# Linear attention before a mixture of experts: block transposes on VectorE, products in quarters of the array, and PSUM in four pairs of banks

## The chip, the core and the metric

The kernel runs on one core of a Trainium2 chip. The metric is the device time of one execution in microseconds (us). A core has five engines with in-order queues of their own: TensorE (PE, its weight loads shown apart as PEld), VectorE (DVE), ScalarE (ACT), GpSimd (POOL) and SyncE (SP, which here only issues DMA transfers). Engines wait for one another by semaphores. TensorE writes into PSUM, 8 banks of 512 fp32 per partition.

## The reference, cut to what matters

Attention first, in fp32, with 8 batches b, 8 heads h, 576 tokens s, head width d = 64 and 128 features f:

```
def phi(x):                                    # x: q or k
    proj = einsum('bhsd,df->bhsf', x, w_phi)
    proj = proj - max(abs(proj), axis=-1)      # one number per token and head
    return concatenate([exp(proj), exp(-proj)], axis=-1)      # 256 features
kv  = einsum('bhsf,bhsd->bhfd', phi(k), v)
z   = sum(phi(k), axis=2)
out = einsum('bhsf,bhfd->bhsd', phi(q), kv) / (einsum('bhsf,bhf->bhs', phi(q), z) + 1e-6)
```

The result, 4608 tokens by 512, goes into a mixture of 8 experts: gate logits, a greedy assignment that gives every expert 576 tokens, and for each expert relu(x @ w1) @ w2.

## The kernel before, in words

There are two stages, one after the other. The attention stage (`attention`, line 90) writes its result to a DRAM array `xs` and leaves the gate logits in an SBUF tile `L`. The expert stage (`moe`, line 508 on, products at lines 813, 842 and 857) gathers rows of `xs` by expert and scatters the output. The change doesn't touch the expert stage.

**The unit.** Attention runs 16 units u; a unit is two batches and two heads, so four (batch, head) pairs of 576 tokens. The steps of a unit, with their lines and short names:

- loads (line 113, on SP's queue): `ki`, `qi`, `vi`, in runs of 1 to 2.3 KB; 10 transfers per unit
- `kt`, `qt` (lines 160, 260): TensorE transposes 9 chunks of 128x128 of k and 9 of q into PSUM, three to a bank; ACT copies them to SBUF (`kh`, `qh`, lines 161 and 261)
- `kg`, `qg` (line 172): the projections on w_phi, 36 products each with 64 rows and 64 columns of the array, a quarter of it; the two heads r go to two banks
- `kgm`, `kgt`, `qgm`, `qgt` (lines 177, 180): DVE takes the largest absolute value per token out of PSUM and subtracts it, 384 numbers per partition an instruction, 24 instructions per unit
- `ke` (lines 191, 192): ACT takes both exponentials of k's projection to `kP`
- `kv` (lines 202, 208): the key-value products, 16 with 128 rows and 64 columns (half the array) and 4 quarters, summed in two banks of their own; ACT copies them out (`kvT`, line 226)
- `ad` (lines 215 to 219): POOL sums phi(k) over the token blocks to `ks`
- `bd` (line 234): kv times a block matrix that holds the identity and the gate weights, 4 full-array products per unit, half of whose operand is zero; ACT copies the result to `kz` (line 237)
- `z`, `zr`, `zc`, `zk` (lines 242 to 250): a product of ones with `ks`, an ACT copy, two TensorE transposes, and a DVE copy into the last column of `kz`
- `T`, `qP` (lines 272, 275): TensorE transposes the projected q, ACT takes both exponentials
- `num` (line 293): phi(q) times `kz`, 72 products per unit, half the array each; the 73 columns are 64 of output, 8 gate logits and the denominator
- `x` (lines 297 to 312): DVE adds 1e-6, inverts, scales logits and output; one transfer per unit to `xs` (line 315)

In the trace each fp32 product of `kg`, `kv`, `bd`, `z` and `num` shows as two MATMUL records, a transpose as one.

**What sets the order.** A planner (`Plan`, lines 18 to 88) places every step on its engine at trace time from a cost, a due time and its buffers. Due times of a unit are offsets (table `ATT`) from u times a pitch `TI`; a change of TensorE's mode (half array `B`, quarter `Q`, full `A`, 32 columns `Z`) carries a penalty, so steps of the same mode are drawn together. PSUM is 6 single banks `g0` to `g5` handed out by the planner, and 2 banks for `kv`. Steps of neighbouring units interleave. Between units run the constants that the expert stage needs (`init`, 40 DVE steps, early) and, after every fourth unit, 12 small routing steps `pr` on DVE and a count on PE (line 499).

Of the kernel before, what the change touches and what calls it, by code (L numbers as in the profile page):

```python
# [89 lines left out]
def attention(ctx, tc, nc, q, k, v, w_phi, w_gate, xs, L, C, xp, cfg={}, after=None, later=None, count=None, init=iter(())):  # L90
# [15 lines left out]
    def load(u,first=lambda: None):
        bp,hp=divmod(u,NP)
        qi=sb.tile([128,2,9,D],F32,name='qi',bufs=2); ki=sb.tile([128,2,9,D],F32,name='ki',bufs=2); vi=sb.tile([128,2,9,D],F32,name='vi',bufs=3)
        T['q',u],T['k',u],T['v',u]=qi,ki,vi
        def put(t,p,s0,s1,x,b,row):  # L110
            n=s1-s0
            o=bass.AP(tensor=x.tensor,offset=x.offset+((b*H+2*hp)*S+row)*D,ap=[[n*D,64],[HS,2],[1,n*D]])
            nc.sync.dma_start(t[p:p+64,:,s0:s1,:].rearrange('p h s d -> p h (s d)'),o)
        b=2*bp
        def kk(t,x):
            put(t,0,0,5,x,b,0)
            put(t,64,0,4,x,b,320)
            if x is k: first()
            put(t,64,4,9,x,b+1,0)
            put(t,0,5,9,x,b+1,320)  # L120
        kk(ki,k)
        for i in range(2): put(qi,64*i,0,9,q,b+i,0)
        kk(vi,v)
# [15 lines left out]
    dv=lambda n,ps_=True: (150 if ps_ else 110)+1.03*n-95
    ac=lambda n,ps_=True: (170 if ps_ else 200)+.83*n-100  # L140
    def unit(u):
# [11 lines left out]
        kof={}
        for i,(c0,c1) in enumerate(ktg):
            n=c1-c0
            for c in range(c0,c1): kof[c]=i
            def pe(x,c0=c0,c1=c1,i=i):
                if c0==0: T['kh',u]=sb.tile([128,9,128],F32,name='kh',bufs=2)
                p=T['ktp',u,i]=bank(('g',u,'kt',i),[128,3,128])(x)
                for c in range(c0,c1): PE.transpose(p[:,c-c0,:],ch(T['k',u],c),ident)  # L160
            def act(x,c0=c0,c1=c1,i=i): A.copy(T['kh',u][:,c0:c1,:],T['ktp',u,i][:,0:c1-c0])
            due=d['kt']+d['ks']*c0/2
            add(('kt',i),'PE',n*109.,due,pe,ld0,'A',slots(('g',NG,'kt',i),*((('khl',2),) if i==0 else ())),(('ki',u),),after=(6000.,9000.,10000.,10200.)[i] if u==0 else 0.)
            add(('kh',i),'ACT',ac(128*n),due+.4,act,(('kt',i),),frees=(('g',u,'kt',i),))
        def project(nm,g,i0,i1,due,deps,src,khl):
            def pe(x):
                P2=T[nm+'p',u,g]=[bank(('g',u,nm,g,r),[128,3,128])(x) for r in range(2)]
                t=T[src,u]
                for i in range(i0,i1):
                    for r in range(2):  # L170
                        for c in range(2):
                            PE.matmul(P2[r][64*c:64*c+64,i-i0,:],t[64*r:64*r+64,i,64*c:64*c+64],C['w'][64*r:64*r+64,:],start=True,stop=True)  # L172
            add((nm,g),'PE',(i1-i0)*222.+55.,due,pe,deps,'Q',slots(('g',NG,nm,g,0),('g',NG,nm,g,1)),(khl,))
            for r in range(2):
                def mx(x,r=r):
                    m=T[nm+'m',u,g,r]=sb.tile([128,3,1],F32,name=nm+'m',bufs=4)
                    V.tensor_reduce(m,T[nm+'p',u,g][r],axis=AX.X,op=OP.max,apply_absolute_value=True)  # L177
                def sub(x,r=r):
                    if g==0 and r==0: T[nm+'t',u]=sb.tile([128,9,2,128],F32,name=nm+'t',bufs=2)
                    V.tensor_sub(T[nm+'t',u][:,i0:i1,r,:],T[nm+'p',u,g][r],T[nm+'m',u,g,r].to_broadcast([128,3,128]))  # L180
# [2 lines left out]
        for g,(i0,i1) in enumerate(PG):
            project('kg',g,i0,i1,d['kg']+d['ks']*1.667*g,[('kh',i) for i in sorted(set(kof[i] for i in range(i0,i1)))],'kh',('khl',u))
        for g,(i0,i1) in enumerate(KG):
            n=i1-i0
            due=d['kg']+d['ks']*g
            def act(x,i0=i0,i1=i1,g=g):
                if g==0: T['kP',u]=sb.tile([128,9,2,256],F32,name='kP',bufs=2)
                kP=fl(T['kP',u][:,i0:i1]); t=fl(T['kgt',u][:,i0:i1])  # L190
                A.activation(kP[:,:,0:128],t,AF.Exp)  # L191
                A.activation(kP[:,:,128:256],t,AF.Exp,scale=-1.0)
            add(('ke',g),'ACT',2*ac(256*n,False),due+2.,act,[('kgs',j,r) for j in pof(i0,i1) for r in range(2)],slot=slots(('kP',2)) if g==0 else (),frees=(('kgt',u),))
        for g in range(1,5):
            np_=len(KV[g])//2
            def pe(x,g=g):
                kP=T['kP',u].rearrange('p c b f -> p (c b) f'); v_=T['v',u]

                if g==1: T['kvps',u]=[ps.tile([128,256],F32,name='kv%d'%i,bufs=1) for i in range(2)]
                for i,b in KV[g]:  # L200
                    a,s_=divmod(b,9); c=a^i
                    PE.matmul(T['kvps',u][i][64*c:64*c+64,:],v_[:,a,s_,:],kP[:,b,:],start=b in (0,5,9,14),stop=False,skip_group_check=True)  # L202
                if g==4:

                    for a in range(2):
                        for i in range(2):
# [1 line left out]
                            PE.matmul(T['kvps',u][i][64*c:64*c+64,:],v_[r,a,4,:],kP[r,9*a+4,:],start=False,stop=True,skip_group_check=True)
# [12 lines left out]
        for a in range(2):
            for i in range(5):
                add(('ad',a,i),'POOL',1330. if i<3 else 780.,d['kv']+d['ks']*(2+2*a)+i*.6,ad(a,i),[('ke',2+2*a)]+([('ad',a,i-1)] if i else []),frees=(('kP',u),),slot=slots(('ks',2)) if a==0 and i==0 else ())
        def kvt(x):
            kt=T['kvT',u]=sb.tile([128,2,256],F32,name='kvT',bufs=2)
            for i in range(2): A.copy(kt[:,i],T['kvps',u][i])
        kend=d['kv']+4*d['ks']
        add(('kvt',),'ACT',2*ac(256),kend+1.,kvt,[('kv',4)],frees=(('kv',u),))
        for i in range(2):
            def pe(x,i=i):  # L230
# [3 lines left out]
                for fh in range(2): PE.matmul(p[:,fh],T['kvT',u][:,i,128*fh:128*fh+128],w,start=True,stop=True)  # L234
# [703 lines left out]
```

## Time and profile before

| | us |
|---|---|
| median of 3 runs (857.64 to 859.37) | 859.0 |
| the profiled execution's own time | 858.03 |
| its span, first to last instruction | 856.3 |
| attention: start to the last transfer to `xs` | 358.6 |
| PE busy in the span | 813.2 |
| DVE busy in the span | 575.3 |
| ACT busy in the span | 383.5 |

The profile is one execution; a row of the timeline merges like instructions that follow each other, gives their start, the time they cover, their count (x48), and in brackets idle time ahead and who ended it. Ends of matmuls are modelled, so the distance from one row's start to the next row's start on the same engine is the better price of a step.

### The profile page before, as it was taken

The page shows a single profiled execution, that of the slowest core. Times are in us where ns is not written, and L with a number is a line of the kernel's source. Part 1 is how long each engine was busy: PE and PEld are TensorE (multiplying, and loading weights), DVE is VectorE, ACT ScalarE, POOL GpSimd, SP SyncE. Part 2 cuts the span into 40 slices and gives each one's busy share as a digit, 9 for nine tenths or more (in the row PEclk, how much of TensorE's full clock was granted, in tenths as well). Part 3 has the DMA queues.
Part 4 walks back from the last instruction along what each step waited for, and adds up shares of the span by engine and source line. Part 5 has one row for each costly group of instructions (what it writes and reads, how often), then busy time and mean ns, then how long its engine had stood idle before and what let it go on. Part 6 is the DMA issues. An engine that isn't in the chain of part 4 may idle for free.

```text
span 856.3 us, 23758 instructions
## 1 busy us (share of the span) xinstructions
PE 813.2 (95%) x9758; PEld 681.7 (80%) x9758; DVE 575.3 (67%) x1727; ACT 383.5 (45%) x852; POOL 262.7 (31%) x302
## 2 busy tenths in 40 slices
PE   5999998999899989769999999999999999999995
PEld 3767886887787878648979879889789798898984
DVE  3987787778777877677858658668667577461410
ACT  3666665666566656403334323333233233251410
POOL 2845555455545544211040130310301202401001
PEclk7999999999999999859999999999999999999998
DMA  8633343554355411114243440532333226610301
GB/s 179 158 94 101 107 121 87 127 129 118 85 132 130 113 45 31 57 62 158 86 142 115 134 144 32 179 129 97 96 117 124 83 102 186 215 62 38 117 13 43
DMA packets 73530, 91.80 MB, mean 107 GB/s; under 512 B 5280, under 2 KB 56512, under 8 KB 73424
## 3 DMA queue, kind: packets, MB, share of 16 engines
q1 hardware_dynamic: 67328, 71.32, 29.5%
q0 software_dynamic: 6096, 18.98, 6.6%
q8 instruction: 77, 1.26, 0.6%
q14 instruction: 29, 0.24, 0.1%
HBM read 71.40 MB, written 18.87 MB: 105 GB/s over the span
## 4 chain that ended last, share of the span: by engine, by line
PE 67%; issue 12%; DVE 12%; DMA 3%; POOL 2%; ACT 2%; SPq 1%; POOLq 0%; ACTq 0%; DVEq 0%
PE h L813 18%; PE y L842 16%; PE g L293 7%; PE g L172 5%; PE kv L202 5%; PE g L272 3%; PE y L857 2%; DVE kgt L180 2%; DVE kgm L177 2%; PE g L260 2%; PE h L788 1%; PE g L160 1%; PE g L234 1%; DVE qgm L177 1%; POOL out_dram L871 1%
## 5 line engine op out<-in xcount | busy, mean ns | idle before, releaser
L813 PE MATMUL h<-xh,w1h 128*128 128x272 f32 (+3 forms) x512 | 144.5, 303 | 0.2 <-DVE xl L791 0.2
L813 PE MATMUL h<-xh,w1l 128*128 128x272 f32 (+3 forms) x512 | 142.9, 299 | 0.0
L824 ACT ACTIVATE fh<-h 128x272 fp32r<-128x272 f32 (+2 forms) x128 | 49.2, 384 | 134.6 <-PE h L813 119.0
L871 POOL DMA_INDIRECT out_dram<-ysb,idx x40 | 40.5, 1012 | 207.1 <-ACT ysb L865 163.6
L842 PE MATMUL y<-w2h,fl 128*128 128x512 f32 x256 | 102.3, 399 | 0.0
L842 PE MATMUL y<-w2l,fh 128*128 128x512 f32 x256 | 101.9, 398 | 0.0
L842 PE MATMUL y<-w2h,fh 128*128 128x512 f32 x256 | 101.4, 396 | 0.0
L813 PEld LDWEIGHTS h<-xh,w1h 128*128 128x128 f32 x512 | 96.4, 189 | 2.1 <-issue 1.2
L813 PEld LDWEIGHTS h<-xh,w1l 128*128 128x128 f32 x512 | 96.6, 189 | 0.0
L783 POOL DMA_INDIRECT xg<-xs,idx x40 | 39.7, 993 | 177.1 <-issue 141.3
L293 PEld LDWEIGHTS g<-kz,qP 128*64 128x64 f32 x2304 | 78.8, 136 | 18.7 <-DVE qgm L177 5.4
L813 PE MATMUL h<-xl,w1h 128*128 128x272 f32 (+3 forms) x512 | 91.7, 298 | 0.0
L828 DVE SCALAR_TENSOR_TENSOR fl<-h,fh 128x272 fp32r<-128x272 f32 (+2 forms) x128 | 52.8, 419 | 56.0 <-ACT fh L824 35.7
L215 POOL TENSOR_TENSOR ks<-kP 128x512 f32<-128x512 f32 x32 | 41.0, 1281 | 156.9 <-issue 132.7
L293 PE MATMUL g<-kz,qP 128*64 128x73 f32 x2304 | 85.7, 228 | 2.1 <-DVE kgt L180 1.1
L177 DVE TENSOR_REDUCE kgm<-g 128x3 f32<-128x384 f32 x96 | 50.8, 550 | 50.2 <-PE g L172 50.0
L275 ACT ACTIVATE qP<-g 128x512 f32<-128x512 f32 (+1 forms) x160 | 81.3, 580 | 6.4 <-PE g L272 6.4
L216 POOL TENSOR_TENSOR ks<-ks,kP 128x512 f32<-128x512 f32 x64 | 81.8, 1278 | 4.8
L813 PEld LDWEIGHTS h<-xl,w1h 128*128 128x128 f32 x512 | 75.6, 188 | 0.0
L191 ACT ACTIVATE kP<-kgt 128x512 f32<-128x512 f32 (+1 forms) x80 | 46.9, 586 | 61.8 <-DVE kgt L180 60.6
L865 ACT COPY ysb<-y 128x512 f32<-128x512 f32 (+1 forms) x40 | 21.8, 544 | 101.7 <-PE y L842 68.4
L202 PE MATMUL kv<-kP,vi 128*64 128x256 f32 x512 | 64.6, 383 | 0.4
(190 smaller groups left out, 1591.9 us busy)
## 6 DMA issues: line engine op xcount, KB each, us to landing
raww<-in_moe_w_dram SPq DMA_DIRECT2D x64, 512.0 KB, 6.2
qi<-in_q_dram SPq DMA_DIRECT2D x32, 288.0 KB, 5.7
xs<-xp SPq DMA_DIRECT2D x16, 576.0 KB, 3.5
ki<-in_k_dram SPq DMA_DIRECT2D x32, 160.0 KB, 3.7
vi<-in_v_dram SPq DMA_DIRECT2D x32, 160.0 KB, 5.2
ki<-in_k_dram SPq DMA_DIRECT2D x32, 128.0 KB, 4.2
vi<-in_v_dram SPq DMA_DIRECT2D x32, 128.0 KB, 5.0
xg<-xs,idx POOLq DMA_INDIRECT x40
```

The source lines that it names most:

```text
L172: PE.matmul(P2[r][64*c:64*c+64,i-i0,:],t[64*r:64*r+64,i,64*c:64*c+64],C['w'][64*r:64*r+64,:],start=True,stop=True)
L177: V.tensor_reduce(m,T[nm+'p',u,g][r],axis=AX.X,op=OP.max,apply_absolute_value=True)
L191: A.activation(kP[:,:,0:128],t,AF.Exp)
L202: PE.matmul(T['kvps',u][i][64*c:64*c+64,:],v_[:,a,s_,:],kP[:,b,:],start=b in (0,5,9,14),stop=False,skip_group_check=True)
L216: elif i<3: G.tensor_add(ks[:,:,a],ks[:,:,a],X(i+1))
L275: for fh in range(2): A.activation(qP[:,fh,0:2*n],X['T'][:,0:2*n],AF.Exp,scale=1.0-2*fh)
L293: PE.matmul(p[64*ab:64*ab+64,j-j0,:],T['qP',u,jj][:,fh,o,64*ab:64*ab+64],T['kz',u,ab][:,fh,a,:],start=fh==0,stop=fh==1)
L813: PE.matmul(p,ws[:,k,o:o+128],xx[:,k,o1:o2],start=n==0,stop=n==11)
L824: A.activation(hh[:,f,o1:o1+m1],p[:,0:m1],AF.Relu)
L828: V.scalar_tensor_tensor(hl[:,f,o1:o1+m1],p[:,0:m1],0.0,hh[:,f,o1:o1+m1],op0=OP.max,op1=OP.subtract)
L842: PE.matmul(p,hx[:,f,o:o+128],ws[:,f%2,:],start=n==0,stop=n==23)
L871: st=G.indirect_dma_start(out=ov,out_offset=bass.IndirectOffsetOnAxis(ap=iv,axis=0),in_=yv,in_offset=None)
```

## The change

It rewrites the attention stage and keeps its units, its results and the expert stage.

- **Transposes.** The 18 TensorE transposes of k and q per unit and their 6 ACT copies go. k and q are loaded (`raw`, line 107) in runs of 32 numbers, 128 bytes, so that partition p of a 32-partition block holds 18 tokens; four VectorE transposes per unit (`blocks`, line 152: 2 for k, 2 for q, 576 numbers per partition each) turn every 32x32 block. 8 transfers per unit for k, 8 for q, 2 for v; for unit 0 half of k's and q's go through ACT's queue.
- **Projections.** Same 72 quarter products; three token blocks go to one pair of banks, so `kgm` and `kgt` handle 768 numbers per instruction, 12 instructions per unit.
- **kv, bd, z in quarters.** `kv` is 36 quarter products into one pair of banks and one copy. `bd` is 16 quarter products with 72 columns, `z` 16 quarter products with 2 columns that land where `zk` copies them: the ACT copy `zr` and the transposes `zc` go.
- **num, x.** Two groups instead of four; DVE scales output and logits in one instruction of 720 or 576 numbers; the sum of logits moves to POOL (`lg`); `xs` is written in runs of 256 bytes by 2 transfers per unit.
- **PSUM.** Four pairs of banks `g0` to `g3` for everything; `vi` has 2 buffers, not 3.
- **Order.** New costs and due times; `kg`, `qg`, `kv`, `bd` and `z` all share mode `Q`.

The core of the diff:

```
-    NG=d['ng']
-    def bank(u_,shape):
-        return lambda x: ps.tile(shape,F32,name='g%d'%x['buf'][u_],bufs=1)
+    NG=4
+    def pair(u_):
+        return lambda x: ps.tile([128,2,512],F32,name='g%d'%x['buf'][u_],bufs=1)
...
+    def raw(eng,t,x,u,bi):
+        bp,hp=divmod(u,NP)
+        for a in range(2):
+            for db in range(2):
+                o=bass.AP(tensor=x.tensor,offset=x.offset+((2*bp+bi)*H+2*hp+a)*HS+32*db,ap=[[18*D,32],[D,18],[1,32]])
+                eng.dma_start(t[64*a+32*db:64*a+32*db+32,bi],o)
...
+        def blocks(nm,aft):
+            for bi in range(2):
+                def f(x,bi=bi):
+                    if bi==0: T[nm+'T',u]=sb.tile([128,2,9,32,2],F32,name=nm+'T',bufs=2)
+                    V.transpose(T[nm+'T',u][:,bi].rearrange('p s t l -> p l s t'),T[nm,u][:,bi])
...
+                for s in range(s0,s1):
+                    for a in range(2):
+                        r=slice(64*a,64*a+64)
+                        for bi in range(2):
+                            PE.matmul(p[64*bi:64*bi+64,a,128*(s-s0):128*(s-s0)+128],t[r,bi,s,:],C['w'][r,:],start=True,stop=True)
...
+                V.tensor_reduce(m,vw(),axis=AX.X,op=OP.max,apply_absolute_value=True)
...
+                            PE.matmul(p[64*a:64*a+64,i,0:256],v_[r,a,s,:],kP[r,s,a,:],start=s==0,stop=s==8,skip_group_check=True)
...
+                            PE.matmul(p[64*c:64*c+64,a,72*(2*i+fh):72*(2*i+fh)+72],t[r,i,o:o+64],C['bd'][r,hp,:],start=True,stop=True)
...
+                            PE.matmul(p[64*c:64*c+64,i,2*(2*fh+a):2*(2*fh+a)+2],ks[r,a,o:o+64],C['one'][r,0:2],start=True,stop=True)
...
-            for i in range(4): PE.matmul(p[32*i:32*i+32,:],C['ones32'],T['ks',u][:,i%2,i//2,:],start=True,stop=True)
-        def zr(x):
-            t=T['zr',u]=sb.tile([128,256],F32,name='zr',bufs=2)
-            A.copy(t,T['zrp',u])
...
+                else: V.tensor_mul(x_[:,:,j0:j1,:],p[:,:,:,0:72],rd.to_broadcast([128,2,n,72]))
+                if g==1:
+                    for a in range(2):
+                        o=bass.AP(tensor=xs.tensor,offset=xs.offset+1152*bp*512+64*(2*hp+a),ap=[[9*512,128],[512,9],[1,64]])
+                        nc.sync.dma_start(o,x_[:,a,:,0:64])
...
-ATT = {'TI': 20.92, 'kt': -4.76, 'kg': 0.32, 'kv': 5.4, 'bd': 1.71, 'z': 7.15, 'zc': 10.93, 'qt': -5.22, 'qg': 7.29, 'T': 9.06, 'num': 28.78, 'stay': 3.25, 'ks': 2.83, 'qs': 3.49, 'ns': 5.37, 'nqP': 6}
+ATT = {'TI': 16.83, 'ldk': 65.46, 'ldq': 71.93, 'ldv': 49.44, 'kt': -9.67, 'kg': -1.7, 'ks': 1.44, 'kv': 7.1, 'kvs': 1.81, 'bd': -4.2, 'z': 0.71, 'qt': -5.11, 'qg': 4.92, 'qs': 1.97, 'T': 4.09, 'num': 17.7, 'ns': 3.45, 'stay': 3.02}
```

How the order moves, at three places in the middle of the attention stage. TensorE before, around one unit's `bd` (g_... are PSUM tiles; x3 counts products; L293 is `num`, L260 `qt`, L160 `kt`, L272 `T`, L234 `bd`, L172 `kg`):

```order
L293 MATMUL g_2656<-kz,qP 64x73 x20
L260 MATMUL g_2684<-ident,qi 128x128 x3
L160 MATMUL g_2694<-ident,ki 128x128 x3
L272 MATMUL g_2699<-ident,qgt 128x128 x4
L234 MATMUL g_2706<-bd,kvT 128x144 x2
L234 MATMUL g_2712<-bd,kvT 128x144 x2
L272 MATMUL g_2716<-ident,qgt 128x128 x4
L160 MATMUL g_2723<-ident,ki 128x128 x3
L260 MATMUL g_2729<-ident,qi 128x128 x3
L272 MATMUL g_2736<-ident,qgt 128x128 x4
```

TensorE now, around one unit's `bd` (L248 is `T`, L220 `bd`, L235 `z`, L169 the projections, L265 `num`, L204 `kv`):

```order
L204 MATMUL g_3100<-kP,vi 64x256 x24
L248 MATMUL g_3163<-ident,qgt 128x128 x6
L248 MATMUL g_3177<-ident,qgt 128x128 x6
L220 MATMUL g_3190<-bd,kvT 64x72 x16
L235 MATMUL g_3218<-one,ks 64x2 x16
L169 MATMUL g_3238<-w,kT 64x128 x12
L248 MATMUL g_3255<-ident,qgt 128x128 x6
L169 MATMUL g_3264<-w,kT 64x128 x12
L169 MATMUL g_3282<-w,kT 64x128 x12
L265 MATMUL g_3300<-kz,qP 64x73 x40
L265 MATMUL g_3361<-kz,qP 64x73 x32
L169 MATMUL g_3405<-w,qT 64x128 x12
```

The transposes of k and q are gone, `num` runs in one block, and the mode changes 94 times over the 16 units where it changed 179 times.

VectorE before, in the same part of the stage (L177 takes the maximum, L180 subtracts it, L297 to L312 are `x`, L250 `zk`):

```order
L177 TENSOR_REDUCE kgm<-g_2741 128x3
L177 TENSOR_REDUCE kgm<-g_2742 128x3
L180 TENSOR_TENSOR kgt<-g_2741,kgm 128x3x128
L180 TENSOR_TENSOR kgt<-g_2742,kgm 128x3x128
L177 TENSOR_REDUCE kgm<-g_2757 128x3
L297 TENSOR_SCALAR rd<-g_2785 128x4
L298 RECIPROCAL rd<-rd 128x4
L302 TENSOR_TENSOR lg<-g_2785,rd 128x32
L312 TENSOR_TENSOR xp<-g_2785,rd 128x4x64
```

VectorE now (L173 the maximum, L176 the subtraction, L269 to L280 `x`, L158 the new transposes, L237 `zk`):

```order
L280 TENSOR_TENSOR xp<-g_4007,rd 128x2x360
L158 STREAM_TRANSPOSE kT<-ki 128x2x288
L269 TENSOR_SCALAR rd<-g_4059 128x8
L270 RECIPROCAL rd<-rd 128x8
L280 TENSOR_TENSOR xp<-g_4059,rd 128x2x288
L173 TENSOR_REDUCE qgm<-g_4106 128x6
L176 TENSOR_TENSOR qgt<-g_4106,qgm 128x768
L173 TENSOR_REDUCE qgm<-g_4134 128x6
L176 TENSOR_TENSOR qgt<-g_4134,qgm 128x768
L158 STREAM_TRANSPOSE qT<-qi 128x2x288 x2
L158 STREAM_TRANSPOSE kT<-ki 128x2x288 x2
L237 COPY kz<-g_4267 128x8
```

Half as many maxima and subtractions of twice the size, with the block transposes of a later unit among them.

SyncE before, the transfers of one unit and the store of an earlier one:

```order
L315 DMA xs<-xp 1152x1x128 [waits DMAHW2_49,DVE_49]
L113 DMA ki<-in_k_dram 64x2x320 [waits DMAHW3_49,PE_49]
L113 DMA ki<-in_k_dram 64x2x256 [waits DMAHW4_49]
L113 DMA ki<-in_k_dram 64x2x320 [waits DMAHW5_49]
L113 DMA ki<-in_k_dram 64x2x256 [waits DMAHW6_49]
L113 DMA qi<-in_q_dram 64x2x576 [waits DMAHW7_49,PE_49]
```

SyncE now, at the same place:

```order
L284 DMA xs<-xp 1152x1x64 [waits DMAHW6_49,DVE_49]
L284 DMA xs<-xp 1152x1x64 [waits DMAHW7_49]
L114 DMA ki<-in_k_dram 32x18x32 [waits DMAHW0_49]
L114 DMA ki<-in_k_dram 32x18x32 [waits DMAHW1_49]
L114 DMA ki<-in_k_dram 32x18x32 [waits DMAHW2_49]
L114 DMA ki<-in_k_dram 32x18x32 [waits DMAHW3_49]
```

A unit now has 18 loads and 2 stores on this queue where it had 10 and 1; in both kernels each waits for the transfer eight places ahead of it.

More of the change, by code (lines that the diff above doesn't have):

```diff
@@ L101, in attention @@
     w=sb.tile([128,512],BF,name='warm',bufs=1); V.memset(w,0.0)
-    p=ps.tile([128,512],F32,name='g0',bufs=1)
-    for _ in range(cfg.get('nwarm',7)): PE.matmul(p,w[:,0:128],w,start=True,stop=True)
+    p=ps.tile([128,2,512],F32,name='g0',bufs=1)
+    for _ in range(cfg.get('nwarm',7)): PE.matmul(p[:,0],w[:,0:128],w,start=True,stop=True)
     T={}
     HS=S*D
-    def load(u,first=lambda: None):
+    C.update(weights(ctx,tc,nc,w_gate,C))
+    def raw(eng,t,x,u,bi):
         bp,hp=divmod(u,NP)
[L108 to L123, printed above, removed]
@@ L153, in unit @@
[L153 to L164, printed above, removed]
@@ L183, in unit @@
[L183 to L193, printed above, removed]
@@ L221, in unit @@
[L221 to L228, printed above, removed]
@@ new lines, in kvt, with bd @@
+        def kvt(x):
+            t=T['kvT',u]=sb.tile([128,2,256],F32,name='kvT',bufs=2)
+            A.copy(t,T['kvp',u][:,:,0:256])
+        kend=d['kv']+2*d['kvs']+1.5
+        add('kvt','ACT',ac(512),kend,kvt,[('kv',2)],frees=(('g',u,'kv'),))
+        def bd(x):
+            p=T['bdp',u]=pair(('g',u,'bd'))(x)
+            t=T['kvT',u]
+            for i in range(2):
+                for fh in range(2):
+                    for a in range(2):
+                        r=slice(64*a,64*a+64)
+                        for c in range(2):
+                            o=128*fh+64*c
+                            PE.matmul(p[64*c:64*c+64,a,72*(2*i+fh):72*(2*i+fh)+72],t[r,i,o:o+64],C['bd'][r,hp,:],start=True,stop=True)
@@ L289, in pe @@
+        lastu=u==NU-1
+        for g,(j0,j1) in enumerate(JG):
+            n=j1-j0; due=d['num']+d['ns']*g
+            js=sorted(set(j//3 for j in range(j0,j1)))
+            def pe(x,g=g,j0=j0,j1=j1):
+                p=T['np',u,g]=pair(('g',u,'num',g))(x)
+                for a in range(2):
                     for j in range(j0,j1):
@@ L316, in unit @@
-                add(('num',a,g),'PE',n*248.,due,pe,[('zk',)]+[('ex',j) for j in js],'B',slots(('g',NG,'num',a,g)),tuple(('qP',u,j) for j in js)+(('kz',u,0),('kz',u,1)))
-                add(('x',a,g),'DVE',760+(90*n if u<NU-1 else 0)+(150 if hp==NP-1 else 0),due+1.6,dve,[('num',a,g)],frees=(('g',u,'num',a,g),))
-        if hp==NP-1 and u<NU-1:
+                                PE.matmul(p[64*ab:64*ab+64,a,73*(j-j0):73*(j-j0)+73],T['qP',u,j//3][:,fh,a,j%3,64*ab:64*ab+64],T['kz',u][:,ab,fh,a,:],start=fh==0,stop=fh==1)
```

256 lines of the change are left out of this document (120 added, 136 removed).

## The prediction, written before the changed kernel ran

> **What bounds the kernel now.** I read the page first: the whole span, the engines' shares, the chain of waits.
>
> ```profile
> span 856.3 us, 23758 instructions
> PE 813.2 (95%) x9758; PEld 681.7 (80%) x9758; DVE 575.3 (67%) x1727; ACT 383.5 (45%) x852; POOL 262.7 (31%) x302
> PE 67%; issue 12%; DVE 12%; DMA 3%; POOL 2%; ACT 2%; SPq 1%; POOLq 0%; ACTq 0%; DVEq 0%
> ```
>
> TensorE holds the kernel. The attention stage is what the change touches, so the next view is the table of busy time by stretch, cut at the first and the last unit's `bd`, and the source view of that line for the two times.
>
> ```profile
> 28.30:347.20 318.90, 307.76 (x5728) 248.52 (x5727) 254.57 (x736) 204.16 (x466) 166.91 (x164) 1.00 0.40 101
> 347.20:358.60 11.40, 9.01 (x203) 7.72 (x201) 5.51 (x31) 8.95 (x31) 0.84 (x2) 1.00 0.18 55
> L234 PE MATMUL g<-bd,kvT x128: 286/286/288, 28.3 to 347.2; 128*128 128x144 f32 x128
> ```
>
> From `bd` of unit 0 to `bd` of unit 15 are 318.9 us, 15 units of **21.26 us**. TensorE is busy 307.8 of them at full clock (1.00), idle 11.1/15 = 0.74 per unit. DVE is busy 254.6/15 = 16.97 per unit, ACT 13.6, and the transfers take 0.40 of the DMA engines. So a unit costs what TensorE costs, and DVE has about 4 us of slack per unit. The pitch times 15 is the term that can move; the tail of 11.4 us and the expert stage behind it have the same work after the change.
>
> **The change part by part: TensorE.** I price steps by the distance between starts in the timeline of one unit (PE rows).
>
> ```profile
> 152.64 1.95 PE L202 MATMUL kv<-kP,vi 128*64 128x256 f32 x16
> 154.52 0.66 PE L208 MATMUL kv<-kP,vi 64*64 64x256 f32 x8
> 155.11 1.49 PE L293 MATMUL g<-kz,qP 128*64 128x73 f32 x40
> ...
> 157.25 0.60 PE L272 MATMUL g<-ident,qgt 128*128 128x128 f32 x4
> 157.68 1.15 PE L234 MATMUL g<-bd,kvT 128*128 128x144 f32 x8
> 158.66 0.60 PE L272 MATMUL g<-ident,qgt 128*128 128x128 f32 x4
> 159.10 0.49 PE L160 MATMUL g<-ident,ki 128*128 128x128 f32 x3
> 159.43 0.49 PE L260 MATMUL g<-ident,qi 128*128 128x128 f32 x3
> ...
> 161.85 0.64 PE L242 MATMUL g<-ks,one 128*32 128x256 f32 x8
> 162.42 1.24 PE L293 MATMUL g<-kz,qP 128*64 128x73 f32 x32
> 163.59 0.55 PE L160 MATMUL g<-ident,ki 128*128 128x128 f32 x3
> 164.82 0.44 PE L248 MATMUL g<-ident,zr 128*128 128x128 f32 x2
> 165.10 0.38 PE L272 MATMUL g<-ident,qgt 128*128 128x128 f32 x2
> 165.41 0.89 PE L172 MATMUL g<-w,qh 64*64 64x128 f32 x24
> 166.11 0.94 PE L172 MATMUL g<-w,kh 64*64 64x128 f32 x24
> 166.99 1.49 PE L293 MATMUL g<-kz,qP 128*64 128x73 f32 x40
> ```
>
> 24 projection records took 0.70 us when more of the same followed (165.41 to 166.11) and 0.88 when another mode followed: a mode change costs 0.17 or so, a quarter record 0.029. Taking 0.17 off groups that end in a mode change: `kv` 1.71 per 16 records, its quarters 0.42 per 8; `num` 1.00 per 32, 0.031 each; `T` 0.43 per 4; `bd` 0.98; `z` 0.40; `zc` 0.28; three transposes of k or q 0.33.
>
> A unit before: projections 144 x 0.029 = 4.20, `kv` 3.42 + 0.42 = 3.84, `T` 18 x 0.108 = 1.94, `num` 144 x 0.031 = 4.46, `bd` 0.98, `z` and `zc` 0.68, `kt` and `qt` 6 x 0.33 = 1.98, and 179/16 = 11.2 mode changes 1.90. Sum 19.98; 1.28 of the pitch is idle time and small gaps.
>
> A unit after:
> - the six transpose groups: gone, -1.98. Their work goes to DVE (below).
> - projections, `T`, `num`: the same records, 10.60.
> - `kv`: 72 quarter records x 0.0525 = 3.78, no change worth naming.
> - `bd` and `z`: 32 quarter records each. No row shows quarters with 72 or 2 columns. Lower bound for `bd`: half the columns over the full array, 0.49; for both, the upper bound is what a quarter record with its own weight load takes in the projection rows, 0.029 x 32 = 0.93. The projection is the nearest row, since each record there, too, loads its own 64 columns of weights, so I take 0.9 for each. That makes `bd`, `z` 1.8 against 1.66 before: the quarters bring nothing here.
> - mode changes: 94/16 = 5.9, 1.00, which is -0.90. This cheapening comes from `bd`, `z`, `kv` and projections sharing one mode.
>
> Sum 10.60 + 3.78 + 1.80 + 1.00 = **17.2 us**. With none of the 1.28 of gaps the pitch is 17.2, with all of them 18.5.
>
> **DVE.** Its rows in the timeline, and one group of the table by line:
>
> ```profile
> 152.13 1.01 DVE L177 TENSOR_REDUCE qgm<-g 128x3 f32<-128x384 f32 x2
> 153.06 1.01 DVE L180 TENSOR_TENSOR qgt<-g,qgm 128x384 f32<-128x384 f32 x2
> ...
> 163.71 0.16 DVE L297 TENSOR_SCALAR rd<-g 128x4 f32<-128x4 f32 x1
> 163.91 0.18 DVE L298 RECIPROCAL rd<-rd 128x4 f32<-128x4 f32 x1
> 164.12 0.22 DVE L302 TENSOR_TENSOR lg<-g,rd 128x32 f32<-128x32 f32 x1
> 164.23 0.41 DVE L312 TENSOR_TENSOR xp<-g,rd 128x256 f32<-128x256 f32 x1
> 164.56 0.55 DVE L180 TENSOR_TENSOR kgt<-g,kgm 128x384 f32<-128x384 f32 x1
> ```
>
> Two instructions of 384 numbers took 0.93, so 0.465 each; 256 numbers took 0.33 (164.23 to 164.56): 1.05 ns per number and 0.06 fixed. 24 x 0.465 = 11.16 become 12 of 768 numbers at 0.87 = 10.44: -0.72. `x` was four times 0.20 + 0.21 + 0.11 + 0.33 to 0.37, 3.5 in all, and becomes 2 x 0.41 + 0.82 (720 numbers) + 0.67 (576) = 2.3: -1.2. The sum of logits goes to POOL; I count nothing for it. Added: four transposes of 576 numbers. No row shows one. Lower bound, no gain being possible from an added instruction, 0.67 at the 1.05 ns; upper bound 0.67 + 0.64, the excess that a DVE instruction with its operand in SBUF showed over the same law when it was slow:
>
> ```profile
> L391 DVE TENSOR_SCALAR kt<-ktf 128x128 bf16<-128x128 f32 x6 | 5.0, 842 | 0.4 <-POOL ktf L390 0.3
> ```
>
> (0.842 for 128 numbers where the law gives 0.20). I take 0.67, since hundreds of rows with the shape of this work follow the law: 4 x 0.67 = +2.7. DVE then needs 16.97 - 0.72 - 1.2 + 2.7 = **17.7 us** per unit, its share of `init` and routing steps included (those 16.97 are busy time, of which merged ends make a few tenths). That is as much as TensorE needs. Two in-order engines that hand work to each other at 17.2 and 17.7 don't reach the larger one exactly; but a share of the DVE work (`init`) lies in the first units only. I take a pitch of **18.1 us**, between 17.2 and 18.5.
>
> A VectorE instruction that waits now also holds the queue: a block transpose waits for its load, and behind it stand the maxima that free PSUM for TensorE. Likewise POOL's `lg` waits for `x`, and behind it the next unit's `ad`. ACT loses six copies, so its 13.6 only falls; four pairs of banks instead of six banks and two are held longer per use, and I count that as part of the 18.1.
>
> **The transfers.** The new ones are 128-byte runs: 2 x 8 x 576 = 9216 per unit, 2304 stores of 256 bytes and 256 runs of 2.3 KB; per DMA engine 576, 144 and 16. The store of unit 15 ran alone, 1152 runs of 512 bytes; the busy shares by stretch give its price. With it the queue's total, and the time SP takes per transfer in the source views:
>
> ```profile
> 359.00:360.00 1.00, 0.64 (x9) 0.62 (x10) 0.89 (x6) 0.00 (x0) 0.00 (x0) 0.80 0.26 79
> 360.00:361.00 1.00, 0.23 (x3) 0.09 (x1) 0.42 (x3) 0.00 (x0) 0.00 (x0) 0.50 1.14 347
> 361.00:362.00 1.00, 0.53 (x14) 0.53 (x15) 0.96 (x5) 0.00 (x0) 0.00 (x0) 0.50 0.59 172
> q1 hardware_dynamic: 67328, 71.32, 29.5%
> L113 SPq DMA_DIRECT2D ki<-in_k_dram x64: 595/610/1082, 0.8 to 293.5; - x64
> L315 SPq DMA_DIRECT2D xs<-xp x16: 513/554/1213, 61.0 to 358.6; - x16
> ```
>
> (0.26 + 1.14 + 0.59) us x 16 engines / 1152 = 27.6 ns for 512 bytes. On queue q1, 29.5% of 16 x 856.3 us over 67328 packets is 60 ns for a mean of 1059 bytes. Twice the bytes cost twice the time, so the price is near to proportional here: a 128-byte run lies between 6.9 ns (in proportion) and 27.6 ns (as a 512-byte run). I take 13, nearer the lower end, for that reason. Then an engine needs 720 x 13 ns + 16 x 130 ns = 9.4 + 2.1 = 11.5 us of 18.1: hidden. SP issues 20 transfers x 0.61 = 12.2 us: hidden. The cover is gone when a short run costs over (18.1 - 2.1)/720 = 22 ns.
>
> **Start and tail.** TensorE's first projection waited for loads, transposes and copies; the new start needs loads of more runs but no ACT copy. I count 0, with 4 us either way: unit 0's k is 288 runs per DMA engine, 4 us more at 27.6 ns than at 13, and about as much may go with the transposes and copies that stood behind one another. Nothing in the tail or behind it changes.
>
> **The sum.** 858.03 - 15 x (21.26 - 18.1) = 858.0 - 47.4 = 810.6, say **811 us**. The profiled execution's 858.03 lies 1 us under the median of 859.0, so I leave the number there. Own range of this case: 858 - 60.9 - 4 = 793 at a pitch of 17.2, 858 - 41.4 + 4 = 821 at 18.5.
>
> **The rivals.**
>
> *DVE becomes the bound.* If a transpose costs the upper 1.31 us, DVE needs 17.7 + 2.6 = 20.3 per unit and everything waits for it: 858 - 15 x 0.96 = 844 us; with stalls at the four pairs alone, any pitch from 18.5 up, so 821 to 844. For it: DVE's slack of 4 us is all used. Against it: 10.4 of its 17.7 us are instructions whose price is well shown. The Trainium skill ("VectorE: DVE Perf Modes", section on the three transpose paths) gives 311 ns for a 128x128 bf16 block transpose; by width, 4.5 of them make 1.40 us for 576 numbers, which would set DVE near 20.6 and the time near 848; no run here shows it.
>
> *The short runs bind: slower.* The place is the 16 DMA engines. If a 128-byte or 256-byte run costs as much as a 512-byte one, 27.6 ns, an engine needs 720 x 27.6 ns + 2.1 = 22.0 us per unit, over the 21.26 of now: 858 + 15 x 0.74 = 869 us, and a late first k adds up to 4. It decides from 26.6 ns up; from 22 ns it eats into the gain. DVE would then idle in front of its transposes. For it: nothing in the trace is as short on this queue. Against it: the near proportion above. The Trainium skill ("DMA: Bandwidth & Descriptors", Specifications) speaks for it: full line rate needs 512 bytes, and below that a transfer becomes a read-modify-write; the trace has no such loads, so it can neither agree nor disagree.
>
> *The change brings next to nothing.* If TensorE keeps its time because waits grow wherever transposes leave, the pitch stays at 20.8 to 21.3: 851 to 859. Against it: TensorE idled only 0.74 per unit with 11 mode changes.
>
> **How the numbers follow.** The forecast (793 to 821) gets 0.51, DVE as the bound (821 to 848) 0.22, short runs 0.18, nothing 0.06, below 793 0.03. Faster by over 0.2% (1.7 us, about what can be told from no change here): 0.51 + 0.22 + 0.03 + 0.01 = 0.77; within 0.2%: 0.03, all of it from the third rival; slower: 0.18 + 0.02 = 0.20. The range leaves out the short runs and the little below 790, and takes in the rest: 790 to 856.
>
> **What would show it.** Right: `bd` rows 18 us apart, PE and DVE both busy above 90% between them, one block transpose near 0.7 us, DMA share 0.6 to 0.7, z's 32 records near 0.9 us. DVE as the bound: transposes above 1 us or PE waiting for `kgt` and `qgt`. Short runs: DMA share near 1 and DVE idle before L158, released by DMA. Wrong altogether: a different time behind the attention stage.

## The result, and the profile after

The changed kernel takes 809.9 us (median of 4 runs, 809.16 to 812.35) against 859.2 us of the kernel before on the same chip (857.64 to 859.58): ratio 0.943, 95% interval 0.941 to 0.946. The prediction said 811. The profiled execution of the changed kernel took 809.45 us. Its page:

```profile
span 807.7 us, 25190 instructions
PE 756.6 (94%) x10718; PEld 653.4 (81%) x10718; DVE 573.1 (71%) x1407; ACT 327.3 (41%) x579; POOL 263.8 (33%) x295
```

TensorE's busy time fell by 56.6 us, the span by 48.6. The table by stretch, cut at each unit's first `bd` (columns: stretch, length, then busy time of PE, PEld, DVE, ACT, POOL with counts, TensorE's granted clock, DMA share, GB/s), shows where; the last row is the whole:

```profile
27.91:50.68 22.77, 19.73 (x443) 17.65 (x442) 19.23 (x31) 9.32 (x13) 14.24 (x17) 0.86 0.76 136
50.68:67.67 16.99, 15.95 (x437) 13.97 (x436) 15.56 (x42) 9.54 (x14) 12.51 (x14) 1.00 0.78 146
67.67:88.55 20.88, 18.24 (x444) 16.11 (x443) 18.84 (x32) 10.28 (x14) 9.19 (x9) 0.92 0.71 135
88.55:107.37 18.82, 17.50 (x450) 14.91 (x449) 16.84 (x26) 11.05 (x16) 11.14 (x12) 1.00 0.76 143
...
124.05:143.42 19.37, 17.49 (x453) 14.81 (x452) 18.20 (x42) 10.30 (x15) 11.44 (x12) 1.00 0.73 135
...
160.20:176.96 16.76, 16.43 (x443) 14.24 (x443) 16.36 (x25) 10.08 (x15) 10.97 (x11) 1.00 0.68 122
...
27.91:301.75 273.84, 257.10 (x6658) 223.57 (x6657) 253.25 (x436) 150.95 (x209) 166.25 (x156) 0.98 0.67 127
```

15 pitches took 273.8 us, 18.26 each, where they took 318.1: 44.2 of the 48.6 us. In a quiet unit (160.20) TensorE and VectorE are both 98% busy. The first four units took 79.5 us, 14.1 more than four times the 16.35 us that turn out below to be TensorE's floor; the three with routing steps 7.6 more; the other eight 6.9 more. Nearly all the rest of the gain lies at both ends: the first `bd` starts at 27.91 us in place of 28.29, and from the last `bd` to the first routing instruction pass 8.1 us in place of 11.4. By TensorE's rows some 2 of these 3.3 us are order: in the kernel before, 32 records of an earlier `num` and 8 more transposes `T` stood there. About 0.8 were `zc` and the waits around it, 0.4 the longer `bd`. That stretch in the changed kernel and in the kernel before:

```profile
301.75:309.88 8.13, 6.90 (x215) 6.41 (x214) 2.17 (x12) 6.78 (x19) 0.92 (x3) 1.00 0.02 4
```

```profile
346.36:357.76 11.40, 9.85 (x210) 8.56 (x208) 5.31 (x28) 8.76 (x28) 1.60 (x3) 1.00 0.18 55
```

### The profile page after: what moved, and what is told of

The parts are those of the page before. It is cut to its first block, busy times and chain, and to the rows that moved or that the text cites. A ratio compares the mean times of both kernels' runs of the same rounds, so it can differ in the third digit from the quotient of the medians.

```text
span 807.7 us, 25190 instructions
## 1 busy us (share of the span) xinstructions
PE 756.6 (94%) x10718; PEld 653.4 (81%) x10718; DVE 573.1 (71%) x1407; ACT 327.3 (41%) x579; POOL 263.8 (33%) x295
## 4 chain that ended last, share of the span: by engine, by line
PE 58%; issue 14%; DVE 10%; POOL 5%; SPq 5%; DMA 4%; ACT 3%; POOLq 0%; DVEq 0%; ACTq 0%
PE h L788 19%; PE y L817 17%; PE g L265 5%; SPq L114 4%; PE g L204 3%; PE g L169 3%; POOL ks L195 3%; PE y L832 2%; PE g L248 2%; ACT qP L252 2%; DMA qi<-in_q_dram 2%; PE h L763 2%; POOL out_dram L846 1%; PE rps L541 1%; DMA ki<-in_k_dram 1%
## 5 line engine op out<-in xcount | busy, mean ns | idle before, releaser
L195 POOL TENSOR_TENSOR ks<-ks,kP 128x512 f32<-128x512 f32 x112 | 142.8, 1275 | 9.9 <-ACT kP L188 1.3
L803 DVE SCALAR_TENSOR_TENSOR fl<-h,fh 128x272 fp32r<-128x272 f32 (+2 forms) x128 | 52.8, 420 | 55.8 <-ACT fh L799 42.4
L188 ACT ACTIVATE kP<-kgt 128x768 f32<-128x768 f32 x96 | 74.5, 835 | 32.9 <-DVE kgt L176 32.5
L265 PE MATMUL g<-kz,qP 128*64 128x73 f32 x2304 | 77.6, 227 | 3.9 <-issue 2.1
L265 PEld LDWEIGHTS g<-kz,qP 128*64 128x64 f32 x2304 | 74.9, 136 | 7.6 <-issue 4.2
L252 ACT ACTIVATE qP<-g 128x768 f32<-128x768 f32 x96 | 71.9, 820 | 11.2 <-PE g L248 11.1
L204 PE MATMUL g<-kP,vi 64*64 64x256 f32 x1152 | 69.7, 382 | 2.4 <-DVE xp L280 1.3
L204 PEld LDWEIGHTS g<-kP,vi 64*64 64x64 f32 x1152 | 48.1, 135 | 13.8 <-issue 2.1
L194 POOL TENSOR_TENSOR ks<-kP 128x512 f32<-128x512 f32 x16 | 20.5, 1280 | 109.2 <-ACT kP L188 109.2
```

The source lines that it names most:

```text
L188: for i in range(2): A.activation(o[:,:,:,128*i:128*i+128],t,AF.Exp,scale=1.0-2*i)
L195: elif s>1: G.tensor_add(ks,ks,kP[:,s])
L204: PE.matmul(p[64*a:64*a+64,i,0:256],v_[r,a,s,:],kP[r,s,a,:],start=s==0,stop=s==8,skip_group_check=True)
L252: for fh in range(2): A.activation(t[:,fh].rearrange('p a s t -> p a (s t)'),p,AF.Exp,scale=1.0-2*fh)
L265: PE.matmul(p[64*ab:64*ab+64,a,73*(j-j0):73*(j-j0)+73],T['qP',u,j//3][:,fh,a,j%3,64*ab:64*ab+64],T['kz',u][:,ab,fh,a,:],start=fh==0,stop=f ...
L803: V.scalar_tensor_tensor(hl[:,f,o1:o1+m1],p[:,0:m1],0.0,hh[:,f,o1:o1+m1],op0=OP.max,op1=OP.subtract)
```

## The experiments

The theory after the result: TensorE's floor per unit fell, and VectorE, filled by the transposes, now stands level with it. The rivals: VectorE alone sets the time; or TensorE still does; or transfers or PSUM do. Of these, transfers are out by the trace alone: from 28 to 302 us of the changed kernel its list of waits names no transfer. All differences below are against the changed kernel, from the ratios to the kernel before, times 859 us; their uncertainty is 2 to 4 us.

### Who sets the time: four kernels on one chip

Edits, on the key-value products (a third of the tokens left out), on the maxima (half of the features left out), and on the transposes (done twice):

```
-                for s in range(s0,s1):            # kv
+                for s in range(s0,min(s1,6)):     # and stop=s==5
-                V.tensor_reduce(m,vw(),...
+                V.tensor_reduce(m,vw()[:,:,:,0:64],...
-                    V.transpose(...)
+                    for _ in range(2): V.transpose(...)
```

> The changed kernel with a third of the key-value products left out (tokens of s = 6, 7, 8 are not summed into kv): 24 of 72 quarter records, which took 1.29 us in the row that starts at 154.09, so TensorE has 1.3 us less per unit; the order on every engine stays. If TensorE alone sets the pitch of 18.26 us: 15 x 1.3 = 19.5 us less, 790 us. If VectorE alone sets it: 810 us, nothing gained. If both are equally full (TensorE 17.1, VectorE 16.9 busy per unit): 2 to 8 us less, 802 to 808.

> The changed kernel with the maxima taken over 64 of the 128 features: six VectorE instructions per unit read 384 numbers in place of 768, 0.47 us in place of 0.87 by the spacing of their starts, 2.4 us less of VectorE per unit; TensorE's work and every order stay. If VectorE alone sets the pitch: up to 15 x 1.5 us less, until TensorE's 17.1 is reached, about 790 us. If TensorE alone sets it: 810 us. If both are equally full: 2 to 10 us less, 800 to 808.

> Both parts left out together: a third of the key-value products (TensorE 1.3 us less per unit) and half the features in the maxima (VectorE 2.4 us less). If both engines are equally full in the changed kernel, only this one gains in full: 15 x 1.3 = 19.5 us or a little more, 785 to 792 us, clearly more than the sum of the two kernels that relieve one engine. If one engine alone sets the time, this gives no more than the kernel that relieves that engine, 790 us at the most.

> The changed kernel with each block transpose issued twice, so that a transpose of 576 numbers costs VectorE 1.4 us in place of 0.7: the price that the second rival of the prediction needed. VectorE then has 16.9 + 4 x 0.69 = 19.6 us per unit. If VectorE is full already, the pitch goes from 18.26 to 19.6 at least and the time to 830 us or above, up to 850 when the early units add to it. If VectorE had room, 810 to 815 us.

| kernel | us | ratio, interval | difference |
|---|---|---|---|
| less TensorE work | 809.5 | 0.943 (0.942 to 0.945) | 0 |
| less VectorE work | 801.5 | 0.934 (0.930 to 0.938) | -8 |
| both | 796.8 | 0.928 (0.926 to 0.930) | -13 |
| transposes twice | 852.5 | 0.993 (0.990 to 0.996) | +43 |

One quiet unit of each, in the order of the table, and of the first and the third kernel their slowest one too:

```profile
180.34:195.88 15.54, 15.06 (x418) 13.21 (x418) 15.12 (x24) 9.36 (x14) 8.96 (x8) 1.00 0.77 146
...
265.29:287.62 22.33, 19.58 (x428) 16.81 (x427) 18.63 (x39) 10.40 (x15) 11.95 (x12) 0.85 0.32 74
```

```profile
174.15:190.50 16.35, 16.35 (x443) 14.18 (x442) 14.05 (x30) 9.88 (x15) 10.84 (x11) 1.00 0.76 144
```

```profile
65.12:87.42 22.30, 17.95 (x419) 16.13 (x418) 15.73 (x32) 10.12 (x14) 10.59 (x12) 0.85 0.76 138
...
273.22:288.29 15.07, 15.07 (x420) 13.29 (x419) 12.90 (x22) 9.90 (x15) 9.02 (x8) 1.00 0.19 42
```

```profile
195.91:216.00 20.09, 16.39 (x442) 14.12 (x442) 19.53 (x32) 9.49 (x14) 10.14 (x9) 1.00 0.78 153
```

With VectorE relieved, TensorE is busy for all of a unit: 16.35 us is its floor. With the transposes doubled, VectorE holds the unit at 20.1 and the whole price lands in the time: 16 x 4 x 0.69 us = 44, measured 43 (the five runs lie between 848 and 854). Neither engine alone is the bound: relieving TensorE gave nothing, relieving VectorE by 2.2 us of busy time per unit gave 8, both gave 13, some 5 more than the two apart, just clear of the uncertainty.

That is less than the 18 to 25 expected of both. The shortfall lies in the first four units: they took 78.5 us, 1.0 less than in the changed kernel, while the other eleven gained 13.3. TensorE waited for VectorE there (4.4 and 3.3 us at the longest), and its granted clock was 0.85, 1.00, 0.85 and 0.91; the row of 22.30 us is one of them. In the kernel with less TensorE work four units (the row of 22.33 us is the slowest) had a clock of 0.84 to 0.92 and took 3.8 us more than the same units of the changed kernel; the other eleven, held by VectorE, gained only 2.2.

### The transposes back on TensorE

```
-                    V.transpose(T[nm+'T',u][:,bi].rearrange(...),T[nm,u][:,bi])
+                    for s in range(s0,s1): PE.transpose(p[:,0,...],T[nm,u][:,s]...,ident)
+                    A.copy(T[nm+'T',u][:,:,s0:s1]...,p[:,0,0:384]...)
```

> The changed kernel with one part undone: k and q are loaded row by row in runs of 256 bytes and transposed by TensorE (18 transposes per unit in groups of three, copied out of PSUM by ACT); quarters, PSUM pairs and planner stay, and the number of mode changes per unit stays 5.9. VectorE loses 2.75 us per unit and TensorE gains 18 x 0.11 = 2.0. If TensorE's time is the floor and VectorE was the nearest behind it: the pitch is 16.4 + 2.0 = 18.4 in the undisturbed units and about 19.5 in the mean, 825 to 835 us. If VectorE alone set the time of the changed kernel: 780 to 805. If six more uses of the four pairs of banks stall both: 840 to 858.

Measured: 842.4 us, ratio 0.981 (0.978 to 0.983), +32 us. A quiet unit, and from TensorE's timeline its `bd` and its three transpose groups:

```profile
197.27:216.92 19.65, 18.83 (x460) 16.08 (x460) 13.43 (x19) 12.70 (x21) 10.52 (x9) 1.00 0.53 122
```

```profile
197.27 0.73 PE L226 MATMUL g<-bd,kvT 64*64 64x72 f32 x32 [0.67 <-ACT kvT L214]
...
198.59 0.87 PE L160 MATMUL g<-ident,qi 128*128 128x128 f32 x6
199.30 0.82 PE L254 MATMUL g<-ident,qgt 128*128 128x128 f32 x6
...
210.96 1.66 PE L160 MATMUL g<-ident,ki 128*128 128x128 f32 x9
212.50 1.55 PE L254 MATMUL g<-ident,qgt 128*128 128x128 f32 x12
213.89 0.49 PE L160 MATMUL g<-ident,qi 128*128 128x128 f32 x3
214.31 1.53 PE L210 MATMUL g<-kP,vi 64*64 64x256 f32 x24
```

The 18 transposes take 0.71 + 1.54 + 0.42 = 2.67 us by their starts, TensorE is busy for 18.83 of the 19.65 us, and VectorE, 13.4 us busy, no longer matters. Of the 0.82 us that TensorE idles, 0.67 are a wait for ACT's copy of `kv`; ACT, with six more copies, is 12.7 us busy where it was 10.1. Moving the transposes off TensorE is the larger part of the gain: 32 of 49 us, net of what it costs VectorE, and with the copies, the loads and the order that go with it.

### Quarters for bd, and the price of a mode change

bd over the full array; then one transpose of the identity inside each projection group, against the same six at the end of the transpose groups:

```
+                    PE.matmul(p[:,i,144*fh:144*fh+144],t[:,i,128*fh:128*fh+128],BD[:,hp],...)  # 4, mode 'A'
+                    if s==s0: PE.transpose(p[:,0,384:512],ident,ident)       # in project
+                PE.transpose(...); PE.transpose(...)                         # control, in tr
```

> The changed kernel with one part undone: the bd product over the full array, four products with 144 columns and a block-diagonal matrix, in place of 16 quarter products. In the kernel before, bd took 0.98 us per unit without its mode change; as quarters it takes 0.58. The planner then has 4.3 mode changes per unit in place of 5.9. If quarters pay by their own price: 0.40 us per unit more of TensorE, less 1.6 x 0.17 = 0.27 for the mode changes, nothing or 2 us, 808 to 812. If the quarters pay through sharing the mode of the projections, as the prediction had it, the other order costs: 812 to 816.

> The changed kernel with two transposes of the identity into unused columns put into each of the six projection groups of a unit, behind the first and the second record group, so that TensorE leaves the quarter mode and comes back: 11.25 mode changes per unit more and the time of the transposes themselves (0.11 us each). If a mode change costs the 0.17 us of the prediction, TensorE gains 1.9 us per unit over the kernel that holds the same transposes inside its transpose groups. With TensorE and VectorE both full the time follows: about 28 us above that kernel. If a mode change costs nothing by itself, the two kernels take the same time.

> The changed kernel with the transposes of the identity put at the end of the three transpose groups of a unit, two in each, where the mode is already theirs: no mode change more, six records of 0.11 us. TensorE gains 0.65 us per unit. If TensorE sets the time of a unit alone or together with VectorE: up to 15 x 0.65 = 10 us more, 815 to 820 us. If VectorE alone sets it: 810 us.

Two transposes in each group are named above, but the kernel holds one, so six per unit, as many as its control. In TensorE's timeline a unit has 18 mode changes (19 with routing steps) where the control has 6 (7), so 12 more and not 11.25.

bd over the full array: 812.1 us, ratio 0.945 (0.942 to 0.948), +1 us, not told apart from the changed kernel. The timeline prices it, here first, then quarters (of the kernel with less VectorE work):

```profile
217.53 1.25 PE L216 MATMUL g<-bd,kvT 128*128 128x144 f32 x8
218.62 1.47 PE L244 MATMUL g<-ident,qgt 128*128 128x128 f32 x12
```

```profile
174.15 0.73 PE L220 MATMUL g<-bd,kvT 64*64 64x72 f32 x32
174.70 0.59 PE L235 MATMUL g<-one,ks 64*64 64x2 f32 x32
175.22 0.89 PE L169 MATMUL g<-w,kT 64*64 64x128 f32 x24
```

1.09 us become 0.55, and a quarter record costs 0.017 us, z's with 2 columns 0.016. The half microsecond is real on TensorE: with `bd` over the full array a quiet unit has 4 mode changes in place of 6, and still TensorE fills 16.88 us of it, 0.5 over the floor of 16.35.

```profile
217.53:234.41 16.88, 16.88 (x420) 14.89 (x419) 15.67 (x24) 9.97 (x14) 8.64 (x9) 1.00 0.74 140
```

Over 15 units that is 8 us, of which the time shows 1, with 2 to 4 of uncertainty. That VectorE, as full, hides the rest fits the four kernels above; no run here shows it by itself.

Mode changes: 832.2 us (ratio 0.968, 0.966 to 0.971) against 814.4 of the control (0.948, 0.947 to 0.950). A quiet unit of the one and of the other:

```profile
189.08:207.96 18.88, 18.88 (x450) 14.95 (x449) 16.53 (x29) 10.07 (x15) 10.48 (x9) 1.00 0.79 149
```

```profile
181.14:198.04 16.90, 16.90 (x449) 14.75 (x448) 15.99 (x28) 10.16 (x15) 10.66 (x10) 1.00 0.77 144
```

TensorE fills both. (18.88 - 16.90) / 12 = 0.165 us for one mode change, with the work otherwise the same. The Trainium skill ("TensorEngine Tiling (Array Packing)", Key Properties) says that a change of mode drains TensorE; these rows agree that it costs time, and give the price. In the time only 17 of 15 x 1.98 = 30 us arrived: the control's mean pitch, 18.44 us, lies 1.5 over its floor, that of this kernel, 19.78, only 0.9 over its own. This fits units that VectorE held anyway.

### Transfers in runs of 64 bytes

```
-                o=bass.AP(...+32*db,ap=[[18*D,32],[D,18],[1,32]])
+                o=bass.AP(...+16*db,ap=[[18*D,32],[D,18],[32,2],[1,16]])
```

> The changed kernel with k and q read in runs of 64 bytes in place of 128: twice as many runs, the same bytes, the same number of transfers; the rows of w are permuted to fit. If a run costs its 13 ns whatever its length, an engine needs 1152 x 13 ns + 2.7 us for the 144 stores of 256 bytes + 2.1 us = 19.8 us per unit, above the pitch of 18.26: the transfers become the bound, 830 to 850 us, and VectorE waits for them in front of its transposes. If the cost goes with the bytes, 6.9 ns: 810 us, nothing changes.

Measured: 859.1 us, ratio 1.001 (0.999 to 1.002): all of the gain is gone, 7.6 us of it ahead of the first `bd`, which starts at 35.47 us in place of 27.91. First the two totals of SP's queue (packets, MB, share of 16 engines), of the changed kernel and of this one; then this one's slowest unit, what TensorE waited for in it, and SP's timeline there:

```profile
q1 hardware_dynamic: 214400, 70.74, 37.5%
```

```profile
q1 hardware_dynamic: 357248, 70.74, 44.4%
```

```profile
136.05:168.25 32.20, 20.57 (x453) 16.47 (x452) 19.58 (x41) 10.30 (x15) 10.80 (x10) 0.79 0.83 111
```

```profile
PE g L204 <- DMA vi<-in_v_dram: 10.7, 1, 10.7
```

```profile
136.58 9.88 SPq L114 DMA_DIRECT2D ki<-in_k_dram  x8
146.56 8.29 SPq L114 DMA_DIRECT2D qi<-in_q_dram  x8
154.94 1.65 SPq L120 DMA_DIRECT2D vi<-in_v_dram  x2
156.69 2.15 SPq L284 DMA_DIRECT2D xs<-xp  x2
```

The same bytes in 142,848 more runs took (0.444 x 859.2 - 0.375 x 807.7) x 16 = 1257 us more of the engines' time, 8.8 ns a run: the price hangs on the number of runs more than on the bytes. But the engines were busy for 0.79 of the stage only. In this stretch the bound was the queue: SP's 20 transfers cover 9.9 + 8.3 + 1.7 + 2.2 = 22 us without a pause, more than the 18.26 of a pitch, and v came late behind k and q. Whether the engines in turn slowed the issue of each transfer is not shown. In the changed kernel the same four kinds already cover 16.1 us:

```profile
141.61 6.15 SPq L114 DMA_DIRECT2D ki<-in_k_dram  x8
147.87 6.47 SPq L114 DMA_DIRECT2D qi<-in_q_dram  x8
154.44 1.32 SPq L120 DMA_DIRECT2D vi<-in_v_dram  x2
155.85 2.20 SPq L284 DMA_DIRECT2D xs<-xp  x2
```

### Three pairs of PSUM banks

`NG=3` in place of 4.

> The changed kernel with three pairs of PSUM banks in place of four, and the order that the planner then finds. The prediction counted the stalls at the four pairs as a part of the 0.9 us between TensorE's sum and the pitch. If the pairs bind already: clearly slower with three, 830 to 860 us. If four were plenty: 810 to 815 us.

Measured: 831.4 us, ratio 0.967 (0.964 to 0.969), +20 us. A quiet unit:

```profile
228.26:246.39 18.13, 17.15 (x443) 14.71 (x442) 16.88 (x25) 10.31 (x16) 10.85 (x10) 1.00 0.66 114
```

Four pairs are not plenty: one fewer, with the order that the planner then finds, costs more than a microsecond per unit. Whether a fifth would gain could not be tried, since PSUM holds four.

### The early units, and a faster kernel

In the changed kernel VectorE waited for an iota that stood on GpSimd behind `ad`, TensorE then for VectorE, and its clock fell. The two waits in the timeline, then TensorE's granted clock (third from the end) in stretches of 1 us:

```profile
41.55 1.28 DVE L366 TENSOR_SCALAR kt<-ktf 128x128 bf16<-128x128 f32 x1 [2.54 <-POOL ktf L365]
44.08 1.48 PE L169 MATMUL g<-w,qT 64*64 64x128 f32 x24 [2.92 <-DVE xp L280]
```

```profile
43.00:44.00 1.00, 0.00 (x0) 0.00 (x0) 0.96 (x3) 0.00 (x0) 1.00 (x1) 1.00 0.71 111
45.00:46.00 1.00, 1.00 (x18) 1.00 (x15) 1.00 (x2) 0.00 (x0) 1.00 (x3) 0.50 0.61 101
...
48.00:49.00 1.00, 1.00 (x24) 0.83 (x16) 1.00 (x3) 0.00 (x0) 0.28 (x1) 1.00 0.57 90
```

The edit sets `init` to 0 and `pitch` to 0.3 (from 25 and 1), so that the constants are made while the first loads are under way; the second kernel also moves `zk` to ACT.

> The changed kernel with the steps that make the constants of the expert stage placed from 0 us of the plan on, 0.3 us apart, in place of from 25 us on, 1 us apart; the work is the same. In the changed kernel VectorE waited 2.54 us for an iota that stood on GpSimd behind the sums of the keys, and 0.87 us for another; the first three pitches after them were 22.8, 17.0 and 20.9 us at granted clocks of 0.86, 1.00 and 0.92, against 16.8 of an undisturbed unit. If these waits and the fall of the clock behind them cost the early units: 7 to 10 us less, 800 to 803 us. If the early units are slow for another reason (the loads, the start of the queue of work): 808 to 811, and the first products may come up to 2 us later.

> The kernel with the early constants (800.2 us) with one more edit: the copy of z into kz goes from VectorE to ACT, 0.15 us less of VectorE per unit. Where VectorE is as full as TensorE, up to 15 x 0.15 = 2 us less: 798 to 800. If the copy now waits behind ACT's exponentials and TensorE's num products wait for it: 802 to 810.

Early constants: **800.2 us**, ratio 0.932 (0.930 to 0.934), 10 us less than the changed kernel and faster than both. Its first three units:

```profile
26.47:47.90 21.43, 19.00 (x455) 15.75 (x455) 19.83 (x29) 10.83 (x15) 12.75 (x11) 1.00 0.71 131
47.90:64.70 16.80, 16.64 (x443) 15.46 (x443) 16.51 (x25) 9.90 (x15) 11.36 (x11) 1.00 0.66 115
64.70:81.22 16.52, 16.52 (x443) 14.88 (x442) 15.99 (x24) 9.95 (x15) 10.53 (x10) 1.00 0.75 143
```

The clock stays at 1.00, and from the second unit on the early units are quiet ones. With `zk` on ACT as well: 808.9 us, ratio 0.943 (0.939 to 0.947), 9 us slower again. Its quiet units take 16.69 us, no less than before, but its three routing units 21.3, 20.1 and 19.9 in place of 19.0, 19.0 and 19.1, and its first unit 23.5: TensorE waited 4.2 us in three waits for the comparison in front of the routing count, 0.5 us without the edit. The planner had reordered those units; why that costs so much was not settled.

## Why the prediction was right

**Pitch.** 18.1 was taken, 18.26 came, but from two errors that cancel. The predicted sum of TensorE was 17.2; its floor is 16.35. Of the 0.85 too much, 0.73 is the term for `bd` and `z`: 0.9 each was taken from the projections' record of 0.029, and 0.55 and 0.52 came, so the step "the quarters bring nothing here" was wrong for TensorE; `bd` came near the lower bound of 0.49 written beside it. In the time it came out right for `bd` (undoing its quarters cost 1 us), most likely because VectorE is as full; `z` was not tried alone. In return the 0.9 us for gaps was too small: 1.9 per unit over the floor, and half of that was not the give and take of two full engines but the early units.

The time of 809 us in the profiled execution, against the forecast of 811, is a second piece of luck. 47.4 us were forecast, all from the pitch, and 44.2 came from it: 2.3 are missing by the 18.26, and 0.8 because the old pitch of 21.26 runs to the last product of `bd` in unit 15; from first product to first product it is 21.20. The tail, forecast at nothing, made up for it. The stated range of 790 to 856 also took in the rival of VectorE as the bound, so it is the rows that tell the two apart: both engines full (TensorE busy 94% of the 15 pitches, VectorE 92%), a transpose near 0.7 us, the DMA share of 0.67, as forecast; only z's 32 records, 0.52 and not 0.9 us, were not. The rival that TensorE keeps its time fell with the 257.1 us that it was busy in 15 pitches, from 306.9.

**Mode changes.** 0.17 each, 5.9 a unit: both as predicted (0.165 by the experiment, and 6 in most units of the timeline).

**VectorE.** 17.7 busy was predicted, 16.9 came (253.25/15). Of the 0.8 too much, 0.4 is the sum of logits, which moved to GpSimd and was counted as nothing: its lines 305 and 307 had 2.2 and 3.9 us of VectorE in the 15 units before. The rest was not traced. The two prices that carried the sum held: one transpose of 576 numbers was taken at 0.67 from the law of other instructions, and its row, with the next one behind it, gives this:

```profile
85.66 0.77 DVE L158 STREAM_TRANSPOSE kT<-ki 128x576 f32<-128x576 f32 x1
86.35 0.92 DVE L173 TENSOR_REDUCE qgm<-g 128x6 f32<-128x768 f32 x1
87.19 0.76 DVE L158 STREAM_TRANSPOSE kT<-ki 128x576 f32<-128x576 f32 x1
87.88 0.92 DVE L176 TENSOR_TENSOR qgt<-g,qgm 128x768 f32<-128x768 f32 x1
88.72 0.94 DVE L173 TENSOR_REDUCE qgm<-g 128x6 f32<-128x768 f32 x1
```

0.69 us by the starts; an instruction of 768 numbers 0.84, where 0.87 was taken. The rival "DVE becomes the bound" fell on its price alone: doubled to 1.4 us the transposes gave 852 us, where 848 had been worked out for 1.40. The estimate of 1.40 us from the Trainium skill's page ("VectorE: DVE Perf Modes", the three transpose paths), scaled from a bf16 figure, was twice what the fp32 rows show here.

**Transfers.** The run of 128 bytes was taken at 13 ns. From 21 to 25 us only such loads were under way:

```profile
21.00:25.00 4.00, 3.02 (x49) 2.09 (x38) 2.48 (x3) 0.81 (x2) 3.77 (x4) 1.00 0.72 113
```

0.72 x 4 us x 16 engines over 113 GB/s x 4 us / 128 bytes is 13.0 ns. So the rival of the short runs fell. The Trainium skill ("DMA: Bandwidth & Descriptors", Specifications) puts the full line rate at 512 bytes and more; the trace agrees that short runs move less, 9.8 bytes per ns and engine against 18.5 in runs of 512 bytes, but a 128-byte run costs half of the 27.6 ns of such a run, not as much, as the rival needed. The DMA share of 0.67 is as predicted. What was mis-sized is SP: 20 x 0.61 = 12.2 us, where 16.1 came. It was hidden, but with 2 us to spare, not 6.

**Start and tail.** The first `bd` moved by 0.4 us, inside the 4 allowed. "Nothing in the tail changes" was wrong by 3.3 us: a part of `num` and of `T`, and `zr` and `zc`, had stood between the last `bd` and the last `num`.

**The account.** Undone by itself, the part with the transposes gives back 32 us. In the 15 pitches the mode changes fell from 11.1 to 6.2 per unit: 15 x 4.9 x 0.165 = 12 us of TensorE, of which the mode experiment's 17 in 30 would let some 7 through, an estimate. With the tail's 3 that makes 42 of 49; the parts were not tried all at once, so the remainder stays unassigned.
